# Sharing out dense matmuls by quota, and waiting for old outputs earlier, at the end of an attention and MLP kernel

## The chip, the cores and the metric

The kernel runs on one core of a Trainium2 chip. The metric is the device time of one execution in microseconds (us). A trace also gives the span, from the first instruction to the last; it is about 2 us shorter. All runs told here were in the fast state, or were single runs, whose state is called unknown; the granted TensorE clock was 0.999 or 1.000 in every one, so no difference below is one of clock.

Engines: PE is TensorE's matmuls, PEld its weight loads, DVE is VectorE, ACT is ScalarE, POOL is GpSimd, SP is SyncE, which here issues the transfers (SPq).

## The reference, cut to what matters

```
xn  = layernorm(x)                                     # x: 2048 x 1024, bf16
out = x + attention(xn, wq, wk, wv, wo, beta) + mlp(xn, w1, b1, w2, b2)

attention: 32 heads of 32, in 4 segments of 512 tokens
  p     = softmax(q k^T * scale + causal mask)         # inside a segment
  a_mem = phi(q) M / (phi(q) z)                        # M, z: memory of the segments before
  o     = g * a_mem + (1 - g) * (p v)
  M    += phi(k)^T v ;  z += sum(phi(k))
  return concat(o) @ wo
```

The MLP comes first in the kernel and is untouched. The change is in the attention, from about 531 us on, and in the last instructions.

## The kernel before

The attention is a loop over 32 units: 4 segments times 8 groups of 4 heads. In unit u PE computes the logits of u and weighs V for unit u-1. Between these it needs other work, because ScalarE takes 1.88 us for each exponential of 128 x 2048 logits, an even unit has three of them, and an odd one two. That other work is a queue of dense jobs. Each job is 8 matmuls of 128 x 512: a Q projection for unit u+2, a V projection, or one half of a chunk of the output projection (`wo_job`). A plan fixes the units of the output projections.

```python
WO_AT = (range(10, 18), (18, 20, 21, 22, 24, 25, 26, 28), (28, 29, 29, 30, 30, 30, 31, 31))

def unit_jobs(self, u):
    jobs = [self.wo_job(*x) for x in self.wo_plan.get(u, ())]   # output projection first
    m = u // 4 + 1
    if m < 2 * N_SEG:
        jobs.append(self.v_job(m, u % 4))
    if u + 2 < N_UNIT:
        jobs.append(self.q_job(u + 2))
        ...                                                     # cut: K
    return jobs

# in the loop over u (cut)
self.jobs.extend(self.unit_jobs(u))
total = 8 * len(self.jobs) - sum(j[0] for j in self.jobs)       # dense matmuls of this unit
cuts = self.cut(total, (0, 4, 2, 4, 1, 13, 8) if even else (7, 3, 2, 4, 1, 15))
self.dense(cuts[0]);        self.logits(u, 0)                   # first logits, exponential
self.dense(cuts[1], end);   self.weigh(u - 1, 0)                # PSUM bank 4
self.dense(cuts[2], False); self.weigh(u - 1, 1)                # PSUM bank 5
self.dense(cuts[3], False); self.weigh(u - 1, 2)                # PSUM bank 4 again
# cut: VectorE's steps of combine(u-1) and phi are queued; dense() emits them between matmuls
self.dense(cuts[4]);        self.logits(u, 1)                   # second logits
if even:
    self.dense(cuts[5]);    self.logits(u, 2)                   # third logits, even units alone
self.dense(100)                                                 # whatever is left of the unit
```

`logits` writes PSUM banks 0 to 3, ScalarE exponentiates them into `pT`, and GpSimd zeroes the part above the diagonal of each block (the mask). `weigh(u-1, 0)` needs the mask of block 1. `weigh` is followed by a VectorE cast out of its bank. Then VectorE scales: `srec`, the product `prod` of 128 x 1024, and `o_s`; SP transposes `o_s` into `oT`, the input of the output projection. Jobs take PSUM banks 6 and 7 in turn. Q and V are copied out by ScalarE; an output projection is added by VectorE to a partial sum, called `fin`, sent out, and the slot is loaded again:

```python
def end(b):                                                      # of wo_job(c, half)
    ...                                                          # cut: fin = bank + fin, on VectorE
    if half == 1:
        self.fw.dma(self.out_d[:, c, :], self.fin[c % 4][:], reads=self.R_fin[c % 4], is_output=True)
        self.load_fin(c + 2)
```

Each of the 54 output transfers has a semaphore of its own. SP waits for all of them at the very end:

```python
def final_waits(self):
    sp = self.E["sp"].eng
    for t in self.out_toks:
        sp.wait_ge(t.sem, t.val)
```

The softmax here doesn't subtract the row's maximum and nothing guards it: scores larger than these inputs give would overflow.

## Time and profile before

| | before |
|---|---|
| time, median of 4 runs (lowest to highest) | 656.27 us (656.05 to 656.65) |
| units 18 to 30, from first logits to first logits of unit 31 | 98.23 us |
| from there to the last landing of an output | 23.31 us |
| from there to the end of the span | 1.35 us |

From the page of the kernel before, the busy times (us, share of the span, instructions) and the chain of work that ended last (shares of the span):

```profile
span 654.1 us, 11147 instructions
...
PE 640.9 (98%) x4560; PEld 302.8 (46%) x4611; DVE 439.7 (67%) x829; ACT 281.2 (43%) x305; POOL 156.1 (24%) x181
...
PE 88%; DVE 7%; issue 2%; ACT 1%; DMA 1%; POOL 0%; DVEq 0%
```

PE is the bottleneck (88% of the chain), but "98% busy" does not tell how much is left, since matmuls overlap. I measured stall like this: take the program's list of matmuls, the usual spacing of starts of each shape (a 128 x 512 matmul starts 215 ns after the one before it, though it lasts 380), and the times of the logits and weighting matmuls, all of which are in the trace. (Some 50 dense records are missing from this trace; the program's list supplies their count.) What a unit takes beyond its list is 0.69 us in an even unit and 0.45 us in an odd one even where nothing waits. I put that down to switching between shapes: in this trace logits start 0.31 us after a dense matmul instead of 0.215, and a dense matmul 0.15 to 0.32 us after a group of logits, whose own starts are 0.003 us apart. Anything above that is called stall below.

First the end of unit 19, in the timeline of the kernel before (columns: start us, duration us, engine, line, operation, out<-in, shapes, count, and in brackets the idle time before and what ended it):

```profile
543.05 0.40 PE L198 MATMUL ps_all<-qT,kT 32*128 32x384 bf16 x8
543.50 1.88 ACT L1361 ACTIVATE pT<-ps_all 128x2048 bf16<-128x2048 f32 x1
543.61 1.67 PE L198 MATMUL ps_all<-xnT,wq 128*128 128x512 bf16 x7 [0.16 <-issue]
545.52 0.40 PE L198 MATMUL ps_all<-qT,kT 32*128 32x512 bf16 x4 [0.24 <-ACT pT L1361]
```

The next logits need banks 0 to 3, so they wait for the exponential that ends at 545.38. Eight dense matmuls (one record is missing) do not cover it.

Second, the end of unit 27 in the same view. The product starts before the mask can; the mask of two blocks takes 2.09 us, and PE's weighting waits for its first block:

```profile
604.34 1.22 DVE L1458 TENSOR_TENSOR prod<-ost,srec 128x1024 bf16<-128x1024 bf16 x1
...
604.73 2.09 POOL L1365 TENSOR_SCALAR_AFFINE_SELECT pT<-pT 128x512 bf16<-128x512 bf16 x2 [2.14 <-ACT pT L1361]
...
606.20 0.25 PE L198 MATMUL ps_all<-vA,pT 128*128 128x33 bf16 x4 [0.24 <-POOL pT L1365]
```

The last pieces of the chain that ended last (start us, us, what): PE waits for the transpose of unit 30, and then come the last adds.

```profile
638.60 2.85 DMA oT<-o_s
641.45 0.05 issue
641.50 2.33 PE ps_all L198 x10
...
647.24 3.60 DVE fin L1611 x7
650.84 0.20 DVEq L318
```

The same place in the timeline, with SP's queue. The issue of a load takes 1.45 us, and the transpose stands behind it:

```profile
637.11 1.45 SPq L220 DMA_DIRECT2D fin<-out_dram  x1
638.60 1.19 SPq L220 DMA_TRANSPOSE oT<-o_s  x1
...
641.50 1.68 PE L198 MATMUL ps_all<-wo,oT 128*128 128x512 bf16 x7 [0.45 <-DMA oT<-o_s]
```

Finally, SP's semaphore instructions, which the timeline does not list, stand in the trace's records: 27 of them, two waits each but the first, and a branch with the last wait, from 651.70 to 653.71 us. Most follow each other after 61 ns; one gap is 0.37 us. The last output landed at 652.77.

### The profile page before, as it was taken

How to read it: one execution, taken by the hardware profiler on the slowest of the kernel's cores; microseconds unless marked ns; L12 is line 12 of the kernel's file. 1: busy time of each engine (PE TensorE's matmuls, PEld its weight loads, DVE VectorE, ACT ScalarE, POOL GpSimd, SP SyncE). 2: the span in 40 equal slices, each digit the busy share in tenths (PEclk: the TensorE clock that was granted, in tenths of full speed). 3: DMA queues.
4: the chain of work that ended last, by engine and by line, in shares of the span. 5: the costliest groups of instructions: out<-in, count | busy, mean ns of one | idle time of the engine just before them, and what ended most of it. 6: DMA issues, size and time to landing. Idle time of an engine off the chain costs nothing.

```text
span 654.1 us, 11147 instructions
## 1 busy us (share of the span) xinstructions
PE 640.9 (98%) x4560; PEld 302.8 (46%) x4611; DVE 439.7 (67%) x829; ACT 281.2 (43%) x305; POOL 156.1 (24%) x181
## 2 busy tenths in 40 slices
PE   8999999999999999999999999999999999999997
PEld 3444444444444444444444444445455444544444
DVE  6975775665655673655637226667988987887885
ACT  7542232232210000111101057778777778889750
POOL 2500000000010221120211203433333445444440
PEclk9999999999999999999999999999999999999999
DMA  9804242242499937718354947989744675454434
GB/s 304 211 0 130 65 114 80 65 127 66 128 265 219 237 88 205 190 67 258 84 173 131 259 118 170 186 178 235 121 107 123 152 164 138 119 102 95 114 86 133
DMA packets 190123, 95.00 MB, mean 145 GB/s; under 512 B 108664, under 2 KB 176248, under 8 KB 190072
## 3 DMA queue, kind: packets, MB, share of 16 engines
q1 hardware_dynamic: 189928, 94.25, 58.1%
q8 instruction: 36, 0.59, 0.4%
q14 instruction: 15, 0.12, 0.1%
q10 hardware_dynamic: 144, 0.03, 0.0%
HBM read 69.23 MB, written 11.53 MB: 123 GB/s over the span
## 4 chain that ended last, share of the span: by engine, by line
PE 88%; DVE 7%; issue 2%; ACT 1%; DMA 1%; POOL 0%; DVEq 0%
PE ps_all L198 88%; DVE prod L1458 1%; DVE ost L1412 1%; ACT pT L1361 1%; DVE fin L1611 1%; DVE ln_st L588 1%; DVE fin L1304 0%; DVE o_s L1464 0%; DMA oT<-o_s 0%; DMA xin<-in_A_x_dram 0%; DVE mtmp L1225 0%; DVE h L628 0%; DVE srec L1454 0%; POOL ln_rs L612 0%; DVE mtmp L1227 0%
## 5 line engine op out<-in xcount | busy, mean ns | idle before, releaser
L1361 ACT ACTIVATE pT<-ps_all 128x2048 bf16<-128x2048 f32 x80 | 150.1, 1876 | 47.8 <-PE ps_all L198 47.6
L1365 POOL TENSOR_SCALAR_AFFINE_SELECT pT<-pT 128x512 bf16<-128x512 bf16 x128 | 107.4, 856 | 160.4 <-ACT pT L1361 160.1
L690 DVE TENSOR_TENSOR part<-ps_all,part 128x512 f32<-128x512 f32 x84 | 57.7, 690 | 108.9 <-PE ps_all L198 88.8
L1076 POOL TENSOR_TENSOR part<-part,stg 128x512 f32<-128x512 f32 x24 | 33.0, 1402 | 285.0 <-DVE part L690 285.0
L747 ACT ACTIVATE g<-part,b1c 128x512 f16<-128x512 f32 x36 | 26.0, 722 | 98.7 <-DVE part L690 98.7
L198 PE MATMUL ps_all<-wv,xnT 128*128 128x512 bf16 x239 | 63.4, 380 | 1.3 <-issue 0.3
L198 PE MATMUL ps_all<-wo,oT 128*128 128x512 bf16 (+2 forms) x255 | 62.0, 366 | 1.8 <-DMA oT<-o_s 0.5
L198 PE MATMUL ps_all<-xnT,wq 128*128 128x512 bf16 x245 | 61.4, 380 | 0.7 <-issue 0.6
L1412 DVE CAST ost<-ps_all 128x396 bf16<-128x396 f32 (+2 forms) x96 | 43.9, 472 | 24.2 <-PE ps_all L198 23.3
L695 ACT ACTIVATE part<-ps_all 128x512 f32<-128x512 f32 x24 | 14.0, 596 | 100.9 <-PE ps_all L198 67.1
L198 PEld LDWEIGHTS ps_all<-vA,pT 128*128 128x128 bf16 x1280 | 45.5, 96 | 20.9 <-DVE ost L1412 3.7
L198 PE MATMUL ps_all<-g,w2s 128*128 128x512 f16 x224 | 51.0, 379 | 0.0
L198 PE MATMUL ps_all<-g,sum 128*128 128x512 f16 x224 | 51.0, 379 | 0.0
L198 PE MATMUL ps_all<-gT,sum 128*128 128x512 f16 x224 | 50.3, 379 | 0.0
L198 PE MATMUL ps_all<-vA,pT 128*128 128x33 bf16 x1280 | 48.5, 177 | 0.6 <-POOL pT L1365 0.2
L198 PE MATMUL ps_all<-h,sum 128*128 128x512 f16 x192 | 45.2, 379 | 0.0
L198 PE MATMUL ps_all<-h,w1s 128*128 128x512 f16 x192 | 44.9, 379 | 0.0
L198 PE MATMUL ps_all<-hT,sum 128*128 128x512 f16 x192 | 43.6, 379 | 0.0
L1458 DVE TENSOR_TENSOR prod<-ost,srec 128x1024 bf16<-128x1024 bf16 x24 | 35.9, 1495 | 0.0
L198 PEld LDWEIGHTS ps_all<-xnT,wq 128*128 128x128 bf16 x256 | 22.8, 97 | 27.3 <-issue 4.9
L198 PEld LDWEIGHTS ps_all<-wo,oT 128*128 128x128 bf16 x272 | 23.1, 97 | 26.0 <-issue 6.1
L198 PEld LDWEIGHTS ps_all<-g,sum 128*128 128x128 f16 x224 | 21.9, 98 | 26.4
(118 smaller groups left out, 859.5 us busy)
## 6 DMA issues: line engine op xcount, KB each, us to landing
w2s<-in_B_w_dram SPq DMA_DIRECT2D x8, 1792.0 KB, 9.4
w1s<-in_B_w_dram SPq DMA_DIRECT2D x12, 1024.0 KB, 5.6
wq<-in_A_wq_dram SPq DMA_DIRECT2D x32, 256.0 KB, 3.3
xs<-in_A_x_dram SPq DMA_DIRECT2D x24, 256.0 KB, 3.5
stg<-in_A_x_dram SPq DMA_DIRECT2D x16, 256.0 KB, 2.9
out_dram<-stg SPq DMA_DIRECT2D x16, 256.0 KB, 3.8
wk<-in_A_wk_dram SPq DMA_DIRECT2D x16, 256.0 KB, 3.5
fin<-out_dram SPq DMA_DIRECT2D x16, 256.0 KB, 3.4
```

What stands on the lines that cost most here:

```text
L198: ins = self.nc.tensor.matmul(*args, **kwargs)
L588: fw.op("dve", lambda e: e.bn_stats(st[:, 6 * h:6 * h + 6], src[:, 512 * h:512 * h + 512]), reads=[self.R_xin[c]], writes=[R])
L690: self.fw.op("dve", lambda e: e.tensor_tensor(self.tmp[dst][:], self.bank(b), self.tmp[src][:], op=ALU.add), reads=[self.R_bank[b], self.R ...
L695: self.fw.op("act", lambda e: e.activation(self.tmp[dst][:], self.bank(b), ACT.Copy), reads=[self.R_bank[b]], writes=[self.R_tmp[dst]])
L747: self.fw.op("act", lambda e: e.activation(self.gB[f % 2][half][:, f // 2, :], src, ACT.Gelu_apprx_tanh, bias=self.b1c[:, f:f + 1], scale= ...
L1076: fw.op("pool", lambda e: e.tensor_tensor(self.tmp[t][:], self.tmp[t][:], self.stg[k][:, 512 * half:512 * half + 512], op=ALU.add), reads= ...
L1361: fw.op("act", lambda e: e.activation(dst, src, ACT.Exp, scale=SCALE), reads=self.R_bank[0:4], writes=[R[v % 2][kb] for v, kb, _ in blocks ...
L1365: fw.op("pool", lambda e: e.affine_select(d, d, pattern=[[0, 4], [1, P]], compare_op=ALU.is_ge, fill=0.0, base=0, channel_multiplier=-1), ...
L1412: fw.op("dve", lambda e: e.tensor_copy(dst, src), reads=[self.R_bank[b]], writes=[self.R_ost[o][part]])
L1458: fw.op("dve", lambda e: e.tensor_tensor(self.prod[:], ost[:, :, 0:D_HEAD], rec.unsqueeze(2).to_broadcast([P, 32, D_HEAD]), op=ALU.mult), ...
L1611: fw.op("dve", lambda e: e.tensor_tensor(dst, self.ps[:, b, c0:c1], dst.bitcast(F16), op=ALU.add), reads=[self.R_bank[b], R], writes=[R])
```

## The change

Its intent is to move waits for outputs that landed long ago off the end, and to give every odd unit from 19 on enough dense work: 24 in even units, 20 in odd ones. The diff, without the counters:

```diff
-    def final_waits(self):
-        sp = self.E["sp"].eng
-        for t in self.out_toks:
+    def wait_outputs(self, but=0):
+        sp, n = self.E["sp"].eng, len(self.out_toks) - but
+        for t in self.out_toks[self.out_waited:n]:
             sp.wait_ge(t.sem, t.val)
+        self.out_waited = n
@@ unit_jobs
-    WO_AT = (range(10, 18), (18, 20, 21, 22, 24, 25, 26, 28), (28, 29, 29, 30, 30, 30, 31, 31))
+    QUOTA_FROM, QUOTA = 18, (24, 20)
-        jobs = [self.wo_job(*x) for x in self.wo_plan.get(u, ())]
+        jobs = [self.wo_job(*self.wo_jobs.popleft())] if 10 <= u < self.QUOTA_FROM else []
         ... V, Q, K jobs ...
+        if u >= self.QUOTA_FROM:
+            quota = self.QUOTA[u % 2] if u + 1 < N_UNIT else 100
+            quota -= 8 * len(jobs) + sum(8 - j[0] for j in self.jobs)
+            while quota > 0 and self.wo_jobs:
+                jobs.append(self.wo_job(*self.wo_jobs.popleft()))
+                quota -= 8
+            self.left = max(-quota, 0)
@@ attention: a job may stay half done for the next unit
-            total = 8 * len(self.jobs) - sum(j[0] for j in self.jobs)
+            total = 8 * len(self.jobs) - sum(j[0] for j in self.jobs) - self.left
-            self.dense(100)
+            self.dense(8 * len(self.jobs) - sum(j[0] for j in self.jobs) - self.left)
@@ tail
             self.load_fin(4 * s + i)
+        fw.wait_outputs(3)
```

The diff has a second effect that is easy to miss. From unit 18 on, output projections now stand behind V and Q, where before they stood ahead. The number of matmuls does not change.

More of the change, by code (lines that the diff above doesn't have):

```diff
@@ L126, in __init__ @@
         self.out_toks = []
+        self.out_waited = 0
         self.own_sems = [ctx.enter_context(nc.semaphore(name=f"s_own{i}"))
@@ L416, in _ @@
             self.attention()
-            self.fw.final_waits()
+            self.fw.wait_outputs()
     def alloc(self):
@@ L1509, in attention @@
     def attention(self):
-        self.jobs, self.turn = deque(), 0
+        self.jobs, self.turn, self.left = deque(), 0, 0
         self.side, self.stops = deque(), self.STOPS
         self.exps, self.in_etmp = [], [None] * 4
-        self.wo_plan = {}
-        for s in range(N_SEG - 1):
-            at = self.WO_AT[s]
-            for n, u in enumerate(at):
-                self.wo_plan.setdefault(u, []).append((4 * s + n // 2, n % 2))
+        self.wo_jobs = deque((c, half) for c in range(4 * (N_SEG - 1)) for half in range(2))
         self.jobs.extend([self.q_job(0), self.k_job(0)] + [self.v_job(0, c) for c in range(4)])
```

## The prediction

-0.9 us from the tail and -0.4 from the units (-1.0 - 0.35 + 0.2 + 0.4 + 0.35) give the forecast of 655.1 us. The two mask times beside the term for unit 26, 1.34 and 0.63 us, are in the trace of the kernel before.

> **What bounds the kernel.** TensorE. The page shows PE busy 98% at a granted clock of 0.999; the chain of waits is 88% PE. [...]a 128x512 matmul lasts 380 ns, but consecutive ones start 215 ns apart. So I summed start-to-start spacings per attention unit and set them against the program's counts times each shape's usual spacing. A unit has a fixed overhead of 0.68 us (even) or 0.45 us (odd) from switching shapes; the rest is stall. Above it, units 18 to 30 (98 us) stall only 3.1 us: units 19, 23, 27 by 0.32, 0.32, 0.54 (the next logits wait for ScalarE's 1.88 us exponential); 20 and 24 by 0.30 and 18 by 0.23 (the weighting waits for a VectorE cast of a PSUM bank, queued behind a 1.65 us product); 28 by 0.42 (GpSimd mask); 30 by 0.61 (output adds on VectorE).
>
> **What the change does.**
> 1. Nothing is removed from PE. Dense matmuls per unit were 24 (even) and 16, 24, 16, 24, 16, 24, 16 (odd, 19 to 31); they become 24 and 20, the last still 16. From 18 on, V and Q jobs stand before output-projection jobs.
> 2. Of 54 output waits at the end, 41 go to the start of the tail, where the SP queue is idle (640.9 to 646.7 us).
>
> **Tail.** In the trace the last output lands at 652.77 us; the end waits, two to an instruction, 61 ns apart, run from 651.70 to 653.71. The 13 left take 0.4 us and are over before the last landing. The difference lies wholly on the critical path: -0.9 us.
>
> **Units.** From the second logits to the next unit's first, the exponential needs about 2.48 us (0.45 start, 1.88, 0.15 release). Eight dense matmuls leave PE there after 2.2 us, nine after 2.4, eleven after 2.84. Units 19, 23, 27 get nine: stall down to about 0.07, together -1.0 us. Units 20, 24, 28 see their VectorE or GpSimd stall shrink by about 0.12 each: -0.35. Against that, units 21, 25, 29 also get nine instead of eleven: +0.07 each. Units 22 and 30 start a job on a PSUM bank whose ScalarE copy (0.6 us) is queued behind that exponential: +0.2 each. Unit 26 meets its mask earlier (one took 1.34 us beside the product, 0.63 alone[...]): +0.35. Net about -0.4 us. All these are estimates.
>
> **Prediction.** 656.36 - 0.9 - 0.4 = 655.1 us, range 653.9 to 656.2. Faster by over 2%: 0.01; within 2%: 0.98; slower by over 2%: 0.01.
>
> **What would show it.** Waits on SP near 641 us and about 7 wait instructions at the end; the span ending 0.45 us after the last landing instead of 1.35. PE stall ahead of the first logits of units 20, 24, 28 nearly gone; small new ones in 22, 26, 30, with waits for ScalarE copies at the first V matmul of 22. Units 19 and 21 lasting alike (5.6 to 5.9 us against 5.24 and 6.44). Matmul counts and busy time unchanged.
>
> **What would make it wrong.** If the new order delays VectorE (an output add now stands before a cast), stalls only move, and only the 0.9 us remain.[...]

## The result, and the profile after

| | before | after |
|---|---|---|
| time, median of 4 runs (lowest to highest) | 656.27 (656.05 to 656.65) | 654.51 (654.28 to 654.63) |
| units 18 to 30 | 98.23 | 97.58 |
| from there to the last landing | 23.31 | 22.85 |
| from there to the end of the span | 1.35 | 0.48 |

The ratio of the fast runs is 0.9972 (95% interval 0.9955 to 0.9989). Ratios are the mean time of one kernel's fast runs over that of the other's of the same rounds, so not quite the ratio of the medians. The three differences in the table, 0.65, 0.46 and 0.87 us, make up the 1.9 us by which the two profiled spans differ (0.07 us of it was lost before unit 18). All outputs are right.

The page after. PE's count is higher only because no matmul record is missing from this trace:

```profile
span 652.2 us, 11204 instructions
...
PE 646.7 (99%) x4611; PEld 303.1 (46%) x4611; DVE 439.9 (67%) x829; ACT 281.5 (43%) x305; POOL 154.9 (24%) x181
...
PE 90%; DVE 4%; DMA 2%; ACT 1%; POOL 1%; issue 1%; DVEq 0%
```

The end of unit 19 in the timeline after. Nine dense matmuls instead of eight follow the second logits, and the profile names no wait any more. By spacing, 0.09 us of stall is left:

```profile
543.76 0.40 PE L199 MATMUL ps_all<-qT,kT 32*128 32x384 bf16 x8
...
544.09 1.25 PE L199 MATMUL ps_all<-xnT,wq 128*128 128x512 bf16 x5
544.21 1.88 ACT L1363 ACTIVATE pT<-ps_all 128x2048 bf16<-128x2048 f32 x1 [1.04 <-PE ps_all L199]
...
545.18 1.03 PE L199 MATMUL ps_all<-wo,oT 128*128 128x512 bf16 x4
...
546.23 0.40 PE L199 MATMUL ps_all<-qT,kT 32*128 32x512 bf16 x4
```

The mask at the end of unit 25, in the same view. This is the pattern of unit 27 before, and it now holds up unit 26 too:

```profile
590.06 1.22 DVE L1460 TENSOR_TENSOR prod<-ost,srec 128x1024 bf16<-128x1024 bf16 x1
...
590.43 2.11 POOL L1367 TENSOR_SCALAR_AFFINE_SELECT pT<-pT 128x512 bf16<-128x512 bf16 x2 [2.55 <-ACT pT L1363]
...
591.92 0.25 PE L199 MATMUL ps_all<-vA,pT 128*128 128x33 bf16 x4 [0.19 <-POOL pT L1367]
```

The tail after, as chain and as timeline. The transpose is no longer a piece of the chain. The load's issue takes 0.92 us instead of 1.45, and no matmul waits for the transpose (a weight load still stands idle for 0.5 us before it, against 0.95):

```profile
636.42 6.38 PE ps_all L199 x67
...
646.21 3.60 DVE fin L1617 x7
649.80 0.20 DVEq L320
```

```profile
636.53 0.92 SPq L221 DMA_DIRECT2D fin<-out_dram  x1
...
637.49 1.19 SPq L221 DMA_TRANSPOSE oT<-o_s  x1
638.73 1.05 SPq L221 DMA_DIRECT2D fin<-out_dram  x2
639.01 3.78 PE L199 MATMUL ps_all<-wo,oT 128*128 128x512 bf16 x16
```

SP's semaphore records show 20 early wait instructions from 639.84 to 640.98 us, and six plus a branch with one more wait at the end. The last output landed at 651.73.

Stall by unit, in us, from the profiled runs (worked out as above):

| unit | 18 | 19 | 20 | 21 | 22 | 23 | 24 | 25 | 26 | 27 | 28 | 29 | 30 | sum |
|---|---|---|---|---|---|---|---|---|---|---|---|---|---|---|
| before | .22 | .32 | .29 | .01 | .00 | .32 | .29 | .00 | .07 | .54 | .42 | .00 | .61 | 3.1 |
| after | .22 | .09 | .10 | .12 | .14 | .10 | .10 | .10 | .42 | .09 | .42 | .09 | .44 | 2.4 |

### The profile page after: what moved, and what is told of

Same layout as the page of the kernel before. It is cut to its first block, busy times and chain, and to the rows that moved or that the text cites. A ratio compares the mean times of both kernels' runs of the same rounds, so it can differ in the third digit from the quotient of the medians.

```text
span 652.2 us, 11204 instructions
## 1 busy us (share of the span) xinstructions
PE 646.7 (99%) x4611; PEld 303.1 (46%) x4611; DVE 439.9 (67%) x829; ACT 281.5 (43%) x305; POOL 154.9 (24%) x181
## 4 chain that ended last, share of the span: by engine, by line
PE 90%; DVE 4%; DMA 2%; ACT 1%; POOL 1%; issue 1%; DVEq 0%
PE ps_all L199 90%; ACT pT L1363 1%; DMA w2s<-in_B_w_dram 1%; POOL pT L1367 1%; DVE fin L1617 1%; DVE ln_st L590 1%; DVE sum L651 0%; DVE prod L1460 0%; DMA xin<-in_A_x_dram 0%; DVE h L630 0%; POOL ln_rs L614 0%; DVE mtmp L1229 0%; DVE mtmp L1227 0%; DVE ost L1414 0%; DVE part L692 0%
## 5 line engine op out<-in xcount | busy, mean ns | idle before, releaser
L199 PE MATMUL ps_all<-wv,xnT 128*128 128x512 bf16 x256 | 68.2, 380 | 0.2
L199 PE MATMUL ps_all<-xnT,wq 128*128 128x512 bf16 x256 | 65.6, 380 | 0.0
L199 PE MATMUL ps_all<-wo,oT 128*128 128x512 bf16 (+2 forms) x272 | 64.3, 367 | 0.2 <-ACT pT L1363 0.2
L199 PEld LDWEIGHTS ps_all<-gT,sum 128*128 128x128 f16 x224 | 21.8, 98 | 26.8 <-DVE gT L666 0.6
L199 PEld LDWEIGHTS ps_all<-g,w2s 128*128 128x128 bf16 x224 | 21.9, 98 | 26.4
```

What stands on the lines that cost most here:

```text
L199: ins = self.nc.tensor.matmul(*args, **kwargs)
```

## The experiments

My theory after the result had three terms: the quota shortens units 18 to 30 by 0.65 us, the early waits cut 0.87 us, and what remains in the tail depends on when the transpose of unit 30 is issued. The rivals were about that third term, about whether the order of jobs matters, and about what holds up the masks. Kernels 1 to 4, 5 to 8 and 9 to 12 ran in three calls; each call timed the kernel before on its own chip, with medians of 655.90, 655.84 and 656.21 us.

### 1. The kernel before again

No edit.

> The kernel before once more, for its trace. Theory (the load issue of chunk 13 just ahead of the transpose of unit 30 is systematically long in this kernel): that issue again lasts about 1.45 us on the SP queue, the transpose is issued near 638.6 us and PE again waits 0.45 us for it in the tail. Rival (chance of that one execution): the issue lasts 0.9 us or less and PE does not wait. The stalls of units 18 to 30 should repeat to 0.05 us in either case; span 654.1 us, or 653.7 by the rival.

Measured: 655.66 us, span 653.9. Every unit's stall repeated to 0.01 us. The load's issue did not repeat: it took 0.43 us, but now the transpose behind it took 1.94. Against the first logits of unit 31 it landed 0.37 us sooner than in the first trace, so PE's wait was about that much shorter. The timeline of this run:

```profile
637.25 0.43 SPq L220 DMA_DIRECT2D fin<-out_dram  x1
...
637.73 1.94 SPq L220 DMA_TRANSPOSE oT<-o_s  x1
```

Neither expectation fits. A fixed long load is wrong, and so is a lucky execution: something held up SP's queue for a while, and whichever issue stood there took the delay. The DMA view has two queues of the kind "instruction", which I take for fetches of instructions. One of them, q8, has 36 packets of 16 KB in the whole run; one of these falls here in every trace, and none of the other queue's does. From the page of the kernel before, and from its DMA view of 636.9 to 638.3 us (packets, MB, share):

```profile
q8 instruction: 36, 0.59, 0.4%
...
q8 instruction: 1, 0.02, 5.5%
```

| trace | fetch ends | the issue it met | that issue ends | difference |
|---|---|---|---|---|
| before | 638.19 | load | 638.56 | 0.37 |
| early waits only (2) | 638.13 | load | 638.49 | 0.37 |
| quota only (3) | 636.76 | load | 637.13 | 0.37 |
| after | 637.07 | load | 637.45 | 0.38 |
| after again (5) | 636.92 | load | 637.29 | 0.37 |
| before again (1) | 638.61 | transpose | 639.67 | 1.06 |
| load later (4) | 638.02 | transpose | 639.09 | 1.07 |

The five other traces in which the load or the transpose met the fetch give 0.35 to 0.38 (four loads) and 1.06 (one transpose). In kernels 7 and 8 the fetch ended before the issue began, and the issue took its plain time: 0.43 for the load, 1.19 or 1.22 for the transpose. Not every issue is held: in nine traces the output's issue just ahead of the load overlapped the same fetch, and it took its plain 0.34 us, even where it began 0.1 to 0.6 us after the fetch had begun. Why it escapes is not known. Over the whole of the 14 traces, 27 issues of a `fin` load began during a fetch or within 0.04 us before one; every one of them ended 0.34 to 0.42 us after it, and 24 took over 0.6 us, where the median of the others is 0.43.

### 2. Early waits only

```diff
 (the kernel before)
+    def wait_outputs(self, but=0): ...          # as in the change
             self.load_fin(4 * s + i)
+        fw.wait_outputs(3)
```

> Only the early waits, old schedule of dense matmuls. Theory (the parts add up, and the tail's transposes are a matter of the schedule): -0.86 us, to about 655.4 us, the end of the span 0.5 us after the last landing, PE's 0.45 us wait for the transpose of unit 30 still there. Rival (moving the waits is what freed the transpose too): -1.3 us, to 655.0 us, and no wait for the transpose.

Measured: 655.23 us, ratio 0.9990 (0.9976 to 1.0003). In the trace the end of the span follows the last landing by 0.48 us instead of 1.35, a cut of 0.87; unit stalls are those of before, and PE still waits for the transpose. The theory holds in the trace. The timed medians differ by 0.67, with an interval as wide as the effect.

### 3. Quota only

```diff
 (the changed kernel)
-        fw.wait_outputs(3)
```

> Only the quota, all output waits at the end as before. Theory: units 18 to 30 shorter by 0.63 us and the wait for the transpose gone, together -1.05 us, to about 655.2 us, with 1.35 us from the last landing to the end of the span. Rival (the transpose was freed by the moved waits): -0.6 us, to 655.65 us, PE still waits 0.45 us in the tail.

Measured: 655.37 us, ratio 0.9990 (0.9977 to 1.0002). The trace: units 18 to 30 took 97.59 us, the end followed the last landing by 1.34 us, and PE did not wait for the transpose. But the profiled run (654.91) was the best of five, the others took 655.34 to 655.41. So the timed gain, 0.5 us, is what the rival said, while the trace shows the theory's. The rival's reason, that the moved waits free the transpose, is refuted by experiment 2.

### 4. The load of chunk 13 behind the transpose

```diff
 (the kernel before; c = 11 is the chunk whose end loads chunk 13)
-                self.load_fin(c + 2)
+                if c != 11:
+                    self.load_fin(c + 2)
@@ tail
-        for i in range(2, 4):
+        for i in range(1, 4):
             self.load_fin(4 * s + i)
```

> The kernel before with one thing moved: the load of the partial sums of chunk 13 is issued after the transpose of unit 30 instead of before it. Theory (the transpose was late because it stood behind that load's issue): the transpose is issued about 1.4 us earlier, near 637.1 us, PE's wait of 0.45 us in the tail is gone, -0.45 us, to 655.8 us. Rival (the transpose itself or its input is late): no change, 656.27 us.

Measured: 655.49 us, 0.41 below before (ratio 0.9993, 0.9980 to 1.0006). The five runs lie within 0.09 us of each other, against 0.72 for the nine runs of the kernel before. The transpose was issued at 637.11 and PE did not wait, although the issue lasted 1.98 us, because it met the fetch. So by the medians the late transpose cost about 0.4 us, though the interval includes no gain; that it was most of the scatter of the kernel before is likely, but not shown.

### 5. The changed kernel again

No edit.

> The changed kernel once more, for its trace and for times on the same chip as the next three. Theory (0.65 us from units 18 to 30, 0.87 us from the end waits; the transpose of unit 30 held up by about 0.4 us on average in both kernels, by an amount that differs from run to run): 1.5 us less than before. The stalls of units 18 to 30 repeat to 0.05 us; the wait in the tail does not. Rival (the freed transpose belongs to the change): 1.9 us less than before.

Measured: 654.12 us against 655.84, ratio 0.9969 (0.9955 to 0.9983). The medians differ by 1.72 us, the means by about 2.0. Unit stalls repeated to 0.02 us. The tail, from the first logits of unit 31 to the last landing, was 22.77 us. With the traces of after and of experiment 3 (22.85, 22.69), the new schedule's mean is 22.77; the three traces of the old schedule and order of loads (23.31, 22.93, 23.25) have a mean of 23.16. My theory, that the tail's scatter is the same in both kernels, falls: the new schedule is 0.4 us better there. The fetch begins 7.06 to 7.31 us after the first logits of unit 31 in these traces, and 7.50 to 8.07 us in the old ones, and SP's load begins at about 7.65 in both. So with the new schedule 0.3 to 0.6 us of the fetch, which lasts 0.88 us in the trace after, is over by then.

### 6. The product waits for the mask

```diff
 (the changed kernel; units 25, 27, 29 compute the product of 24, 26, 28)
-            fw.op("pool", lambda e: e.affine_select(d, ...
+            mask = fw.op("pool", lambda e: e.affine_select(d, ...
+            if kb == 1:
+                self.mask1 = mask
@@ products
-                  reads=R_ost + [R_rec], writes=[self.R_prod])
+                  reads=R_ost + [R_rec], writes=[self.R_prod], extra=[self.mask1] if u in (24, 26, 28) else [])
```

> The changed kernel with one wait more: in units 25, 27 and 29 the VectorE product waits until GpSimd has masked the first block. Theory[...]: that mask lasts 0.63 us instead of 1.34, and the 0.42 us stall ahead of the first weighting of units 26, 28 and 30 is gone; since the product starts about 1 us later, a new stall of 0.4 to 0.6 us for the cast of the PSUM bank stands in the same units, so the span changes by less than 0.5 us. Rival (the mask is late because ScalarE's exponential ends late): the mask still ends where it did and the stall ahead of the first weighting stays at 0.4 us.

The timeline of this run at the end of unit 25:

```profile
590.23 1.22 POOL L1367 TENSOR_SCALAR_AFFINE_SELECT pT<-pT 128x512 bf16<-128x512 bf16 x2 [2.55 <-ACT pT L1363]
...
590.89 1.63 DVE L1462 TENSOR_TENSOR prod<-ost,srec 128x1024 bf16<-128x1024 bf16 x1 [0.96 <-POOL pT L1367]
...
591.36 0.26 PE L199 MATMUL ps_all<-vA,pT 128*128 128x33 bf16 x4
```

The masks took 1.22 us for two blocks instead of 2.11, and PE's weighting did not wait for them. ScalarE's exponential ended as before, so the rival is refuted: the product was what held the mask. But the product now took 1.63 us instead of 1.22, and it began later. The stalls of units 26 and 28 only went from 0.42 to 0.38, now as waits for VectorE's cast, unit 29's rose from 0.09 to 0.22, and unit 30's from 0.44 to 1.56. One run took 655.09 us, about 1 us more than the changed kernel, twice what I had expected as the worst.

### 7. The second logits earlier

```diff
 (the changed kernel)
             self.dense(cuts[3], False)
+            early = u % 2 == 1 and u >= 25
+            if early:
+                self.logits(u, 1)
             if u:
                 self.weigh(u - 1, 2)
@@
-            self.logits(u, 1)
+            if not early:
+                self.logits(u, 1)
```

> The changed kernel with the second logits of units 25, 27, 29 and 31 moved ahead of the third weighting group, so that ScalarE starts that exponential about 0.7 us earlier against PE. Theory (nine dense matmuls do not cover the exponential, and the mask meets the product because the exponential ends just after the product starts): the 0.09 us stalls of 25, 27, 29 and the 0.42 us stalls of 26, 28, 30 go, the tail's 0.24 us wait for the exponential goes, and up to 0.15 us per unit returns as waits for VectorE: about -1.3 us against the changed kernel. Rival (the stalls are VectorE's and only move): less than 0.4 us.

Measured: 655.31 us, ratio 0.9986 (0.9973 to 0.9998), so about 1.2 us slower than the changed kernel. I expected 1.3 us faster. The stalls of 25 and 27 went, those of 26 and 28 fell to 0.24, but 29's rose from 0.09 to 0.13, unit 30's to 1.42, and the tail got 0.5 us longer. From the timeline of this run, around units 25 and 30:

```profile
589.98 1.67 POOL L1367 TENSOR_SCALAR_AFFINE_SELECT pT<-pT 128x512 bf16<-128x512 bf16 x2 [1.87 <-ACT pT L1363]
590.11 1.04 DVE L1229 SCALAR_TENSOR_TENSOR pqT<-qT,mtmp 128x512 bf16<-128x512 bf16 x1
...
591.07 1.65 DVE L1460 TENSOR_TENSOR prod<-ost,srec 128x1024 bf16<-128x1024 bf16 x1
...
623.25 0.57 PE L199 MATMUL ps_all<-vA,pT 128*128 128x33 bf16 x16 [0.68 <-DVE ost L1414]
```

The masks now come first and lengthen two VectorE operations: `pqT` from 0.69 to 1.04 us, and the product from 1.22 to 1.65. That makes 0.8 us more VectorE time, and by unit 30, where output adds come on top, PE waits for VectorE. The rival, that the stalls move, was nearer; they even grew.

### 8. Both: earlier logits, and the load behind the transpose

Edits of 7 and 4 together.

> The same with the load of chunk 13 issued after the transpose of unit 30. Theory: another 0.3 to 0.5 us off, and the times of its runs closer together (within 0.15 us) than those of the changed kernel: about 2.9 to 3.3 us less than before in all, near 653 us. Rival (the transpose is held up wherever it stands): no further gain.

Measured: 654.46 us, ratio 0.9974 (0.9961 to 0.9986), runs within 0.22 us. It is 0.85 us better than 7 alone, but not better than the changed kernel (654.12), and far from the 653 that I expected. In 7 the output's issue and the load came 0.9 us later against unit 31 than in the other traces, so the transpose behind them was late (PE waited 0.54 us for it) although no fetch held them; here that wait is gone.

### 9. Moving the instruction fetch

```diff
 (the kernel before; matmuls on zeros at the very start, before any input is there)
-            for _ in range(self.N_WARM):
-                fw.mm(self.bank(0), self.warm[:, 0:P], self.warm[:], start=True, stop=True)
+            for i in range(self.N_WARM + 21):
+                n = 64 if i < 24 else 512
+                fw.mm(self.bank(0)[:, 0:n], self.warm[:, 0:P], self.warm[:, 0:n], start=True, stop=True)
```

(The fetch meant is the 16 KB packet of q8 from 636.96 to 638.19 us. That it is of TensorE's instructions, and that it moves by 3 to 5 us, were assumptions.)

> The kernel before with nothing moved in the attention: of the 15 warming matmuls at the very start, three are replaced by 24 of 64 columns, so that TensorE's instruction stream is 42 instructions longer[...]. Theory (the SP queue's transfer issue that meets such a fetch ends 0.37 us after the fetch ends): the fetch seen at 637 us moves to 632 to 634 us, the load of chunk 13 is issued in 0.43 us and the transpose of unit 30 in 1.19, PE does not wait for it, -0.4 to -0.6 us against before. Rival (the fetch only happens to lie there): the issues stay 0.2 to 1.0 us too long and PE waits as before.

Measured: 655.48 us, ratio 0.9989 (0.9976 to 1.0003), medians 0.73 us apart. Units 18 to 30 took 98.24 us, as before. The timeline of this run:

```profile
637.05 0.47 SPq L220 DMA_DIRECT2D fin<-out_dram  x1
...
637.57 1.19 SPq L220 DMA_TRANSPOSE oT<-o_s  x1
...
639.54 2.75 PE L198 MATMUL ps_all<-wo,oT 128*128 128x512 bf16 x12
```

The load was issued in 0.47 us and PE did not wait for the transpose. The fetch did move, by less than I expected: it ran from 636.11 to 637.16 us, so it still touched the load's issue, which ended 0.37 us after it. Nothing else in the attention was changed, and the tail took 22.67 us instead of 22.93 to 23.31, so the position of the fetch makes the difference of 0.3 to 0.6 us in the traces; the interval of the timed runs includes no gain. The other traces in which the load met the fetch bear this out, whatever their schedule: ordered by the end of the fetch after the first logits of unit 31, 7.75 (this run), 7.94, 8.00, 8.09, 8.14, 8.18, 8.61, 8.73 and 8.80 us, their tails are 22.67, 22.69, 22.70, 22.77, 22.84, 22.85, 23.25, 23.31 and 23.40 us. The fetch began 6.70 us after the first logits of unit 31, which is 0.8 to 1.4 us earlier than in the old schedule's other traces; why not 3 us or more, I do not know.

### 10. The order alone

```diff
 (the kernel before)
-        jobs = [self.wo_job(*x) for x in self.wo_plan.get(u, ())]
+        wo = [self.wo_job(*x) for x in self.wo_plan.get(u, ())]
+        jobs = [] if 18 <= u < 28 else wo
         ... V, Q, K jobs ...
+        if 18 <= u < 28:
+            jobs += wo
```

(A first build that did this from 18 to 31 stopped at an assertion of the kernel's own: Q of unit 30 was finished before its slot for the exponential was free.)

> The kernel before with its old counts of dense matmuls (24, and 16 or 24), but V and Q jobs ahead of the output projection in units 18 to 27. Theory (the counts made the gain, not the order): stalls of 0.32, 0.32 and 0.54 us stay in units 19, 23 and 27, about 0.3 in 20 and 24, none in 22 or 26 beyond 0.1, units 18 to 30 together within 0.15 us of the kernel before (98.23 us). Rival (the order frees VectorE): the stalls of 20 and 24 fall to 0.1 and the sum by 0.4 us or more.

Measured: 656.73 us (one run), units 18 to 30 took 98.62 us, 0.4 longer than before, so outside the 0.15 that I expected. The stalls of 19 and 23 stayed at 0.31 and those of 20 and 24 at 0.30, as the theory said, and 27's fell to 0.31. Units 22 and 28 got 0.36 and 0.66. In this one trace the order alone brings no gain, and costs a little.

### 11. The quota with the old order

```diff
 (the changed kernel)
-            while quota > 0 and self.wo_jobs:
-                jobs.append(self.wo_job(*self.wo_jobs.popleft()))
-                quota -= 8
+            wo = []
+            while quota > 0 and self.wo_jobs:
+                wo.append(self.wo_job(*self.wo_jobs.popleft()))
+                quota -= 8
+            jobs = wo + jobs
```

> The changed kernel with its counts (24 and 20), but the output projection ahead of V and Q as before the change. Theory (the counts made the gain): stalls of about 0.1 in 19, 21, 23, 25, 27, 29, about 0.1 in 20 and 24, 0.15 in 22, 0.4 in 26, 28 and 30, units 18 to 30 together within 0.15 us of the changed kernel (97.59 us). Rival (the order is needed): 0.4 us or more longer.

Measured: 655.97 us (one run). Up to unit 28 every stall equals the changed kernel's to 0.03 us. Units 29 and 30 have 0.60 and 1.72 us instead of 0.09 and 0.44, and units 18 to 30 take 99.34 us, 1.8 longer than in the changed kernel. The timeline of this run in units 29 and 30 shows how:

```profile
618.84 0.69 DVE L1306 TENSOR_TENSOR fin<-ps_all,fin 128x512 bf16<-128x512 f32 x1 [0.43 <-PE ps_all L199]
619.45 0.19 DVE L1455 TENSOR_TENSOR srec<-ost,eps 128x32 f32<-128x32 bf16 x1
...
621.58 1.65 DVE L1460 TENSOR_TENSOR prod<-ost,srec 128x1024 bf16<-128x1024 bf16 x1
...
624.53 0.57 PE L199 MATMUL ps_all<-vA,pT 128*128 128x33 bf16 x16 [0.79 <-DVE ost L1414]
```

With the projection first, its output add stands ahead of the scaling in VectorE's queue and waits for PE; the product starts at 621.58. In the changed kernel the add stands behind the product, which starts at 619.39. So my expectation fails for the last two units: there the order is needed.

### 12. The changed kernel with the load behind the transpose

The edit of 4 on the changed kernel.

> The changed kernel with the load of chunk 13 issued after the transpose of unit 30: the proposed best version. Theory: 0.1 to 0.4 us below the changed kernel, that is 1.8 to 2.2 us below before, with runs within 0.15 us of each other. Rival: no gain.

Measured: 654.15 us against 656.21, ratio 0.9970 (0.9957 to 0.9982), runs within 0.28 us. Experiment 5 gave 0.9969. No gain can be told apart, as the rival said. No version tried beats the changed kernel.

## Why the prediction was right or wrong, point by point

The measured 654.51 us lies in the range 653.9 to 656.2, 0.6 us below the predicted 655.1. The forecast change was -1.3 us (from 656.36, the median of the three runs then on record), the measured one -1.76. The range reaches almost to the kernel before, so lying in it proves little; the terms do. The two main ones held, several small ones were off or had the wrong sign, and one term was missing.

- **"Tail ... -0.9 us" by early waits.** Right. 0.87 us in the trace, and again 0.87 with the waits alone (experiment 2).
- **"Units 19, 23, 27 get nine: stall down to about 0.07, together -1.0 us."** Right: 0.09, 0.10, 0.09, together -0.90.
- **"Units 20, 24, 28 see their ... stall shrink by about 0.12 each."** The sum was right by luck, the parts were not: 20 and 24 shrank by 0.19 each, 28 not at all. Experiments 10 and 11 show that the counts shortened 20 and 24, not the order: the order alone left them at 0.30, and the quota with the old order gave 0.1. The mask still met the product there (the pattern shown for unit 25).
- **"Units 21, 25, 29 ... +0.07 each."** Right: 0.11, 0.10, 0.09.
- **"Unit 26 meets its mask earlier: +0.35."** Right: +0.35. Experiment 6 shows that the product holds the mask (two blocks in 2.11 us with the product first, in 1.22 with the mask first).
- **"Units 22 and 30 ... +0.2 each."** Right in size for 22 (+0.14), where the V matmuls began at 561.56 and the ScalarE copy before them ended at 561.41; no run tested that link alone. Wrong in sign for 30: it fell from 0.61 to 0.44. I had overlooked that the new order puts an output add of unit 29 behind the product; experiment 11 shows that the old order costs unit 30 1.3 us here.
- **"Net about -0.4 us"** for the units: -0.65.
- **The missing term.** The prediction sums only end waits and units. The tail shrank by another 0.4 us (mean of three traces each), because a fetch of instructions no longer holds up SP's queue ahead of the transpose of unit 30 as long (the load's issue took 0.92 us instead of 1.45). I had read PE's 0.45 us wait for the transpose, but not asked what made the issue ahead of it last 1.45 us. Experiments 4 and 9 each remove that wait on the old schedule; their traced tails are 22.68 and 22.67 us, and they gain about 0.4 and 0.7 us by the medians, with intervals that include no gain.

The three terms, 0.65, 0.87 and 0.4, sum to 1.9 us; the medians gave 1.76 and, on another chip, 1.72. What stays open is why the new schedule puts the fetch about 0.5 us earlier against unit 31. It does so without exception: 7.02 to 7.31 us after its first logits in the eight traces with the quota, 7.50 to 8.07 in the five with the old schedule, experiment 9 apart. PE's records show four more semaphore instructions ahead of unit 31 with the quota (123 instead of 119; experiment 10 has 118). Whether these four move the fetch, no run tested; the 42 more instructions of experiment 9 moved it by 0.8 to 1.4 us. The quota alone does it in its one trace, yet four of its five timed runs were 0.45 us slower than the traced one, so it may not do so in every execution.

## What to carry to other kernels

When PE is nearly full, do not read its headroom from busy time (98% here, with matmuls of 380 ns that start 215 ns apart): count the matmuls between two fixed points of the program, compare with the spacing of starts, and name each wait above that. Evening out filler work paid here where a fixed latency, about 2.48 us from the second logits until their exponential has freed the banks, was not covered; the order of the filler can matter as much (1.8 us in experiment 11), because each job brings an eviction that queues on another engine (there a 0.69 us add on VectorE). Where VectorE was busy 82 of 98 us, freeing GpSimd a little earlier cost more than it gained (about 1 us more in all in experiment 6, 1.2 in 7). An issue on a transfer queue that takes several times its usual length (1.45 us here instead of 0.43) is a wait like any other: ask what held it, and look at the instruction fetches too.

## What the traces showed of the hardware

- Of the two queues of the kind "instruction", q8 moved 36 packets of 16 KB. That they are TensorE's instructions is my inference from experiment 9. In the 12 traces where the load or the transpose on SP's queue met such a fetch in the tail, its issue ended 0.35 to 0.38 us (a load) or 1.06 to 1.07 us (a transpose) after the fetch ended; in the first trace of the kernel before this made the load's issue 1.45 us instead of 0.43. An output's issue that overlapped the same fetch kept its plain 0.34 us.
- `prod` on VectorE and the masks on GpSimd were longer beside each other: the mask took 1.34 instead of 0.63 us when the product was first, the product 1.63 instead of 1.22 us when the mask was first (experiment 6). `pqT` on VectorE took 1.04 instead of 0.69 us beside the masks (experiment 7).
- SP's waits that were already met stood two to an instruction, and most of these instructions followed each other after 61 ns.
